# A block-sparse attention and squared-ReLU kernel: new one-hot table, shorter mask chain, a second output bank, and the third query tile of batch 0 masked on VectorE

## The chip, the cores and the metric

The kernel runs on one core of one Trainium2 chip. The metric is the device time of a run in microseconds (us); lower is better. PE is TensorE, ACT is ScalarE, DVE is VectorE, POOL is GpSimd, SP is SyncE, which issues most of the loads.

## The reference

Attention for 4 batches x 8 heads, 768 positions of 64 numbers, under a mask of 32x32 blocks: the band around the diagonal, the first and last block row and column, and three sampled blocks for each block row. Its output, 3072 x 512, goes through two matrices with a squared ReLU between them.

```python
scores = scale * np.matmul(q, k.transpose(0, 1, 3, 2))
...
scores = np.where(mask, scores, -1000000000.0)
scores = scores - np.max(scores, axis=-1, keepdims=True)
attn = np.exp(scores)
attn = attn / (np.sum(attn, axis=-1, keepdims=True) + 1e-09)
...                       # np.matmul(attn, v), then per token:
h = x @ w_in
r = np.maximum(h, 0.0)
g = r * r
return (g @ w_out).astype(np.float32)
```

## The kernel before

A unit is two heads of one batch; a batch has four units. A unit has three query tiles of 256, and a query tile has three key pairs (2 x 128 keys). For each key pair PE makes scores, ACT exponentials `pT`, and PE multiplies them with V into an output bank `po`. After three key pairs ACT takes the inverse of the sums (two Ln, one Exp) and DVE normalises into `xT`. Only then is the bank free. When all four units have normalised a query tile, its hidden matmuls `ph` can run, which fill PE wherever attention leaves it idle.

In batch 0 the mask is not there yet. PE adds it to the scores with four further matmuls a key pair, from a one-hot table `oh` and mask rows `bq`. From batch 1 on, DVE multiplies `pT` with a finished mask.

```python
add = u < HP and qi < NQ_ADD            # NQ_ADD = 3: all of batch 0
for c in range(2 if add else 0):
    for h, hs in enumerate(HALVES):
        nc.tensor.matmul(ps[:, h, c, :], oh[hs, ksl[c]], bq[hs, qsl], start=c == 0, stop=False, ...)
for c in range(2):
    for h, hs in enumerate(HALVES):
        nc.tensor.matmul(ps[:, h, c, :], KT[i][hs, ksl[c]], QT[i][hs, qsl], start=not add, stop=True, ...)
...
otile[u, qi] = ps_o.tile([P, 2, QW], F32, name="po", tag="po")      # one bank: bufs=1
...
def inverse(u, qi):                     # ACT: Ln, Ln, Exp
def normalize(u, qi):                   # DVE: two multiplies out of po; then the bank is free
```

The order of instructions on each engine is not written by hand. The kernel records tasks with assumed durations, landing times and priorities, and a list scheduler in the kernel issues them. So one changed number can move the order of everything after it.

The softmax here doesn't subtract the row's maximum and nothing guards it: scores larger than these inputs give would overflow.

Of the kernel before, what the change touches and what calls it, by code (L numbers as in the profile page):

```python
# [25 lines left out]
def kernel(  # L26
# [94 lines left out]
    def run_schedule(free, bufs, ring):  # L121


        taken = {name: [] for name in bufs}
        left = {e: [t for t in tasks if t.eng == e] for e in free}
        while any(left.values()):
            best = None
            for e, ts in left.items():
                cand = [(max(r, free[e]), t) for t in ts
                        for r in (t.ready(taken, bufs),) if r is not None]  # L130
                if cand:
                    at = min(c[0] for c in cand)
                    t = min((c[1] for c in cand if c[0] <= at + 1e-9), key=lambda t: (t.key, t.order))
                    if best is None or at < best[0]:
                        best = (at, t)
            assert best is not None, "no task can start"
            at, t = best
            t.end = t.issued = free[t.eng] = at + t.us
            if t.dma:
                t.end = ring[t.eng] = max(ring[t.eng], t.end) + t.dma  # L140
            if t.get:
                taken[t.get].extend(t.bufs)
            for p in t.put:
                p.holds -= 1
                p.free = max(p.free or 0.0, t.end + t.late)
            left[t.eng].remove(t)
            t.fn()
        return max(free.values())
# [32 lines left out]
    load_part(nc.sync, 0, 1, 1, CP)  # L181
    load_part(nc.sync, 0, 2, 0, CP)
    load_part(nc.sync, 1, 1, 0, CP)
    load_part(nc.sync, 1, 0, 0, 1)
    load_part(nc.sync, 1, 2, 0, CP)
# [22 lines left out]
    col = consts.tile([nb, nb], F32, name="col")  # L208
    row = consts.tile([nb, 1], F32, name="row")
    small = dict(allow_small_or_imprecise_dtypes=True)  # L210
    G.iota(rel, pattern=[[1, nb]], base=0, channel_multiplier=-1, **small)
    G.iota(col, pattern=[[1, nb]], base=0, channel_multiplier=0, **small)
    G.iota(row, pattern=[[0, 1]], base=0, channel_multiplier=1, **small)


    warm = consts.tile([P, 512], BF, name="warm")
# [3 lines left out]
    def warm_up(n):  # L220
        nc.tensor.matmul(pw[:, 0:n], warm[:, 0:P], warm[:, 0:n], start=True, stop=True)  # L221

    for _ in range(4):
        warm_up(512)
# [4 lines left out]
    key = consts.tile([P, S], mybir.dt.int16, name="key")  # L229
    ends = consts.tile([P, 2], F32, name="ends")  # L230
    oh = consts.tile([P, S], BF, name="oh")
    for hs in HALVES:
        G.iota(ends[hs, 0:1], pattern=[[0, 1]], base=0, channel_multiplier=block, **small)
    G.iota(key[:, 0:2 * P], pattern=[[1, 2], [NCH, P]], base=0, channel_multiplier=0, **small)
    identb = consts.tile([P, P], BF, name="identb")
    make_identity(nc, identb)
    G.iota(key[:, 2 * P:S], pattern=[[1, NCH - 2], [NCH, P]], base=2, channel_multiplier=0, **small)

    def one_hot(n0, n1):
        cols = slice(n0 * P, n1 * P)  # L240
        V.tensor_scalar(out=oh[:, cols], in0=key[:, cols], scalar1=ends[:, 0:1], scalar2=None, op0=AOP.is_ge)
        V.scalar_tensor_tensor(out=oh[:, cols], in0=key[:, cols], scalar=ends[:, 1:2], in1=oh[:, cols],
                               op0=AOP.is_le, op1=AOP.mult)


    sbf = consts.tile([nb, n_rand], F32, name="sbf")
    edge = consts.tile([nb, 2], F32, name="edge")
    pm = ps_h.tile([nb, 4, nb], F32, name="pm", tag="h")
    V.tensor_scalar(out=pm[:, 0, :], in0=rel, scalar1=-1.0, scalar2=None, op0=AOP.is_ge)
    V.scalar_tensor_tensor(out=pm[:, 1, :], in0=rel, scalar=1.0, in1=pm[:, 0, :],  # L250
                           op0=AOP.is_le, op1=AOP.mult)
    V.tensor_scalar(out=edge[:, 0:1], in0=row, scalar1=0.0, scalar2=None, op0=AOP.is_equal)
    V.tensor_scalar(out=edge[:, 1:2], in0=row, scalar1=float(nb - 1), scalar2=None, op0=AOP.is_equal)
    V.tensor_scalar(out=pm[:, 0, :], in0=pm[:, 1, :], scalar1=edge[:, 0:1], scalar2=edge[:, 1:2],
                    op0=AOP.max, op1=AOP.max)
    V.memset(pm[:, 0, 0:1], 1.0)
    V.memset(pm[:, 0, nb - 1:nb], 1.0)
    V.tensor_scalar(out=ends[:, 1:2], in0=ends[:, 0:1], scalar1=float(block - 1), scalar2=None, op0=AOP.add)
    one_hot(0, 2)
    bm = consts.tile([nb, 2, D], BF, name="bm")  # L260
    V.memset(bm, 0.0)
    V.tensor_copy(out=sbf, in_=sb_i.rearrange("q (r two) -> q r two", two=2)[:, :, 0])
    cur = 0
    for r in range(n_rand):
        V.scalar_tensor_tensor(out=pm[:, 1 - cur, :], in0=col, scalar=sbf[:, r:r + 1],
                               in1=pm[:, cur, :], op0=AOP.is_equal, op1=AOP.max)
        cur = 1 - cur
    V.tensor_scalar(out=bm[:, :, 0:nb], in0=pm[:, cur:cur + 1, :].broadcast_to([nb, 2, nb]), scalar1=-1.0,
                    scalar2=-NEG, op0=AOP.add, op1=AOP.mult)
# [6 lines left out]
    def rows_product(qi):  # L276
        pb = ps_y.tile([P, QW], F32, name="pb", tag="y")
# [6 lines left out]
    def mask_product(qi, cp):  # L284
        pq = ps_y.tile([P, 2, QW], F32, name="pq", tag="y")
# [13 lines left out]
    def cast_qk(eng, u, w, c0, c1):  # L299
# [3 lines left out]
        eng.tensor_copy(out=c[:, ns], in_=raw[u][w][:, :, ns, :].rearrange("p t n d -> p n t d"))  # L303
# [74 lines left out]

    def values(u, qi, cp):
        i = u % NPB  # L380
        pT = ptile.pop((u, qi, cp))
        if cp == 0:
            otile[u, qi] = ps_o.tile([P, 2, QW], F32, name="po", tag="po")
# [94 lines left out]
    for u in (2, 3):  # L478
        load_part(nc.sync, u, 1, 0, CP)
        load_part(nc.sync, u, 0, 0, 1)  # L480
        load_part(nc.sync, u, 2, 0, CP)
# [3 lines left out]
    for i in range(HP):  # L485
        init_v(G, i)

    NQ_ADD = 3
# [3 lines left out]
    land_k = [(3.0, 4.4), (6.7,), (9.3,), (12.0,)]  # L492
    land_q = [(3.5, 13.8, 15.3), (7.1, 14.2, 15.7), (9.7, 14.6, 16.1), (12.4, 14.9, 16.5)]
    land_v = [5.6, 8.2, 10.9, 13.5]
# [15 lines left out]
    wu = [Task("PE", 0.2, 1e6, (lambda: warm_up(256)), get=None if i else "po") for i in range(10)]  # L510
# [4 lines left out]
    oh_t = Task("DVE", 1.0, 0.5, (lambda: one_hot(2, NCH)), after=5.6, **SEM)  # L515
    rc = []
    for qi in range(NQ):
        rp = Task("PE", 0.2, -7 if qi == 0 else 12 * qi - 6, (lambda qi=qi: rows_product(qi)), get="y",
                  deps=[oh_t] if qi else [], after=7.0 * qi, **pe)
        rc.append(Task("ACT", 0.4, -7 if qi == 0 else 12 * qi - 6, (lambda qi=qi: rows_copy(qi)), deps=[rp], put=[rp], **SEM))  # L520
    for qi in range(NQ):
        for cp in range(CP):
            s = HP * CP * NQ_ADD + (qi - 2) % NQ * CP + cp - 6
            t = Task("PE", 0.27, s, (lambda a=(qi, cp): mask_product(*a)), deps=[rc[qi]],
                     get="y", after=13.0 + 2.5 * ((qi - 2) % NQ * CP + cp), **pe)
            mk[qi, cp] = Task("DVE", 0.62, s, (lambda a=(qi, cp): mask_copy(*a)), deps=[t], put=[t], **SEM)

    def prepare_first(u):
# [4 lines left out]
        for w, c0, c1, at, s in parts:  # L533
            n = c1 - c0
            a = (u, w, c0, c1)
            on = "POOL" if c0 and not w else "DVE"
            c = Task(on, 0.06 + (0.17 if on == "DVE" else 0.36) * n, s - 6,
                     (lambda a=a, e=G if on == "POOL" else V: cast_qk(e, *a)), get="qc", after=at, **SEM)
# [42 lines left out]
    N_ONE = 72  # L581

    def attend(s, slots):
# [4 lines left out]
        for j, a in enumerate(slots):  # L588
# [4 lines left out]
            if u >= HP or qi >= NQ_ADD:  # L593
                mm = Task("DVE", 0.82, k - 1, (lambda a=a: mask_mul(V, *a)), deps=[ex, mk[qi, cp]], **SEM)
            va = Task("PE", 0.44, k + 2.2, (lambda a=a: values(*a)), deps=[mm] + cv[u] + va_all[-1:],
                      get=None if cp else "po", put=[ex], **pe)
# [10 lines left out]
    while s < len(order):  # L607
        slots = order[s:s + (1 if s < N_ONE else 2)]
# [49 lines left out]
    run_schedule({"PE": 3.0, "DVE": 3.9, "ACT": 3.2, "POOL": 6.2, "SP": 10.5},  # L658
# [32 lines left out]
```

## Time and profile before

| | before |
|---|---|
| median time | 320.81 us (320.67 to 321.29, 3 runs) |
| profiled span | 319.4 us |
| PE, ACT, DVE, POOL busy | 306.7, 226.7, 203.3, 176.9 us |
| first exponential | 8.73 us |
| first hidden matmul | 39.09 us |

A busy PE is not a PE at its peak: matmuls overlap, so the busy time of PE also covers latency. The Trainium skill says so in "Perfetto Trace Analysis", Identifying the Most-Contended Engine: matmul busy time is not a good measure of how close PE is to its peak. The trace agrees: a value matmul is recorded with 0.27 us, while the next one starts after 0.109. I therefore add a second reading, worked out from the trace. Each matmul gets its cost back to back, as spacings in the traces show it: 0.0545 us for a 64-row matmul (scores and mask adds run in pairs), 0.109 for 128 rows by 256 columns, 0.163 by 384, 0.216 by 512, 0.056 for a transpose, and 0.105 for each change between 64-row, 24-row and full-array matmuls. At any moment, the time passed less the cost of all matmuls issued so far is **PE time lost**. Warm-up matmuls and the three row products count as lost. Span is then PE work plus lost time plus about 4 us of tail: for this kernel 296.4 + 19.0 + 4. Each such account rests on one profile of a kernel. In the profiles of x5 and of x7 to x13 below, 31 to 33 of the 384 output matmuls (`py`) have no record; the lost times given for them count each of these at 0.216 us.

The view that I had not shown in the prediction, and should have, is the ACT timeline reduced to the first step of each inverse. It marks one turn of the output bank (start, length):

```profile
15.13 0.38 ACT L398 ACTIVATE ls<-po 64x256 f32<-64x256 f32 x1
21.21 0.38 ACT L398 ACTIVATE ls<-po 64x256 f32<-64x256 f32 x1
27.26 0.38 ACT L398 ACTIVATE ls<-po 64x256 f32<-64x256 f32 x1
32.80 0.38 ACT L398 ACTIVATE ls<-po 64x256 f32<-64x256 f32 x1
```

The inverses, and with them the turns, are 6.08, 6.05 and 5.54 us apart, although a unit holds only 3 x 0.967 + 1.13 = 4.03 us of ACT work.

### The profile page before, as it was taken

Reading aid. Unit: us, or ns where it says so; the run is one execution under the profiler, and the core shown is the slowest. Engines: PE = TensorE matmul, PEld = TensorE weight load, DVE = VectorE, ACT = ScalarE, POOL = GpSimd, SP = SyncE. Lnnn points to the kernel's source line nnn. Section 1 sums busy time; section 2 is a strip of 40 time slices with the busy share of each in tenths; the row PEclk is TensorE's granted clock in tenths of the full one; section 3 lists DMA queues with packets and bytes.
Section 4 is the critical chain, followed back from the end, with each engine's and each line's share of the span. In section 5 each row is a group of like instructions: output and inputs, shape, how many; then the busy total and the mean of one; then the engine's idle time right before and its main releaser. Section 6 shows DMA issues by size and latency. Waiting matters only on the chain.

```text
span 319.4 us, 6150 instructions
## 1 busy us (share of the span) xinstructions
PE 306.7 (96%) x2339; PEld 174.2 (55%) x2339; DVE 203.3 (64%) x369; ACT 226.7 (71%) x362; POOL 176.9 (55%) x227
## 2 busy tenths in 40 slices
PE   6989899999999999999999989999999999999995
PEld 3555466565655545555555545656555655555542
DVE  7644464485886977888896759786667676332200
ACT  2799978885898998778878688796878687311111
POOL 8560533384866636987664538835354445565620
PEclk9999999999999999999999999999999999999999
DMA  7996699117735735735700253620000000000002
GB/s 227 337 210 144 138 180 197 41 27 205 192 90 182 197 77 158 207 74 183 197 33 35 49 184 64 195 57 33 2 35 33 2 34 33 36 33 33 35 33 99
DMA packets 42597, 34.47 MB, mean 108 GB/s; under 512 B 20680, under 2 KB 39624, under 8 KB 42568
## 3 DMA queue, kind: packets, MB, share of 16 engines
q1 hardware_dynamic: 37928, 29.63, 32.4%
q0 software_dynamic: 4224, 4.19, 8.2%
q8 instruction: 18, 0.29, 0.4%
q10 hardware_dynamic: 416, 0.26, 0.3%
q14 instruction: 11, 0.09, 0.1%
HBM read 27.26 MB, written 6.29 MB: 105 GB/s over the span
## 4 chain that ended last, share of the span: by engine, by line
PE 81%; ACT 9%; DVE 6%; issue 4%; DVEq 0%; ACTq 0%
PE ph L426 24%; PE py L456 22%; PE po L389 11%; PE ps L365 10%; PE po L391 9%; ACT pT L371 5%; PE ps L361 3%; DVE pT L376 2%; DVE r L437 1%; ACT ls L399 1%; ACT ls L398 1%; ACT rs L400 1%; PE pw L221 1%; PE pt L314 1%; DVE xT L410 0%
## 5 line engine op out<-in xcount | busy, mean ns | idle before, releaser
L443 POOL TENSOR_TENSOR g<-r 128x384 bf16<-128x384 f32 (+1 forms) x144 | 130.3, 915 | 100.3 <-DVE r L437 73.4
L371 ACT ACTIVATE pT<-ps 128x1024 bf16<-128x1024 f32 x144 | 142.5, 1020 | 35.8 <-PE ps L365 28.7
L426 PE MATMUL ph<-xT,w_in_sb 128*128 128x384 bf16 (+1 forms) x576 | 118.9, 309 | 1.8 <-DVE r L437 1.6
L456 PE MATMUL py<-w_out_sb,g 128*128 128x512 bf16 x384 | 109.2, 379 | 0.7 <-ACT ys L463 0.7
L376 DVE TENSOR_TENSOR pT<-pT,mask 128x1024 bf16<-128x1024 bf16 x108 | 88.5, 834 | 20.4 <-ACT pT L371 19.0
L437 DVE TENSOR_SCALAR r<-ph 128x384 f32<-128x384 f32 (+1 forms) x98 | 49.7, 513 | 50.4 <-PE ph L426 40.1
L426 PEld LDWEIGHTS <-w_in_sb 128*128 128x128 bf16 x576 | 53.3, 98 | 46.3 <-issue 12.1
L389 PE MATMUL po<-pT,VA 128*128 128x256 bf16 x288 | 71.3, 275 | 2.3 <-ACT pT L371 1.6
L391 PE MATMUL po<-pT,VB 128*128 128x256 bf16 x288 | 70.7, 273 | 0.0
L365 PE MATMUL ps<-QT,KT 64*128 64x256 bf16 x576 | 50.4, 274 | 0.0
L456 PEld LDWEIGHTS <-g 128*128 128x128 bf16 x384 | 37.2, 98 | 23.9 <-issue 1.0
L389 PEld LDWEIGHTS <-VA 128*128 128x128 bf16 x288 | 28.0, 97 | 25.9 <-issue 13.9
L435 ACT ACTIVATE r<-ph 128x384 f32<-128x384 f32 (+1 forms) x46 | 20.7, 450 | 23.9 <-POOL g L443 17.1
L365 PEld LDWEIGHTS <-KT 64*128 64x128 bf16 x576 | 22.5, 95 | 20.8 <-issue 18.6
L391 PEld LDWEIGHTS <-VB 128*128 128x128 bf16 x288 | 28.2, 98 | 6.6
L409 DVE TENSOR_TENSOR xT<-po,rs 64x256 bf16<-64x256 f32 x48 | 19.8, 412 | 12.6 <-ACT rs L400 12.4
L398 ACT ACTIVATE ls<-po 64x256 f32<-64x256 f32 x48 | 18.2, 380 | 8.6 <-PE po L391 7.6
L463 ACT COPY ys<-py 128x512 f32<-128x512 f32 x23 | 13.3, 584 | 12.7 <-PE py L456 12.7
L303 POOL CAST qc<-qs 128x768 bf16<-128x768 f32 (+1 forms) x20 | 15.2, 771 | 11.8 <-DMA qs<-in_q_dram 10.1
L400 ACT ACTIVATE rs<-ls 128x256 f32<-128x256 f32 x48 | 20.0, 417 | 1.5
L410 DVE TENSOR_TENSOR xT<-po,rs 64x256 bf16<-64x256 f32 x48 | 20.5, 428 | 0.6
L308 POOL CAST VA<-vs 128x384 bf16<-128x384 f32 x16 | 10.8, 672 | 16.9 <-PE po L389 9.4
(52 smaller groups left out, 116.7 us busy)
## 6 DMA issues: line engine op xcount, KB each, us to landing
vs<-in_v_dram SPq DMA_DIRECT2D x16, 384.0 KB, 5.2
out_dram<-ys SPq DMA_DIRECT2D x23, 256.0 KB, 2.2
ks<-in_k_dram SPq DMA_DIRECT2D x15, 384.0 KB, 4.5
qs<-in_q_dram SPq DMA_DIRECT2D x12, 384.0 KB, 3.6
w_in_sb<-in_moe_w_in_dram POOLq DMA_DIRECT2D x4, 512.0 KB, 10.0
w_out_sb<-in_moe_w_out_dram POOLq DMA_DIRECT2D x4, 512.0 KB, 9.5
qs<-in_q_dram SPq DMA_DIRECT2D x12, 128.0 KB, 5.1
ks<-in_k_dram SPq DMA_DIRECT2D x1, 256.0 KB, 3.1
```

Of the source, the lines that this page charges most:

```text
L365: nc.tensor.matmul(ps[:, h, c, :], KT[i][hs, ksl[c]], QT[i][hs, qsl], start=not add, stop=True, skip_group_check=True)
L371: nc.scalar.activation(out=pT, in_=stile.pop((u, qi, cp)), func=AF.Exp, scale=scale)
L376: eng.tensor_mul(out=pT, in0=pT, in1=mask[:, None, qi, cp * 2:cp * 2 + 2, :].broadcast_to([P, 2, 2, QW]))
L389: nc.tensor.matmul(po[:, 0, :], VA[i][:, n, :], pT[:, 0, c, :], start=first, stop=last, skip_group_check=True)
L391: nc.tensor.matmul(po[:, 1, :], VB[i][:, n, :], pT[:, 1, c, :], start=False, stop=last, skip_group_check=True)
L398: nc.scalar.activation(out=ls[0:D, :], in_=po[D:P, 0, :], func=AF.Ln)
L400: nc.scalar.activation(out=rs, in_=ls, func=AF.Exp, scale=-1.0)
L426: nc.tensor.matmul(ph, w_in_sb[:, kc, f * P:(f + 1) * P], xT[b][:, kc, c0:c0 + w], start=(kc == 0), stop=(kc == KM - 1))
L435: nc.scalar.activation(out=r, in_=htile.pop((T, f)), func=AF.Relu)
L437: V.tensor_scalar(out=r, in0=htile.pop((T, f)), scalar1=0.0, scalar2=None, op0=AOP.max)
L443: G.tensor_mul(out=g, in0=r, in1=r)
L456: nc.tensor.matmul(py, gtile[T, f][:, ts * P:(ts + 1) * P], w_out_sb[:, f, :], start=(f == 0), stop=(f == NF - 1))
```

## The change

It has three parts. *The start*: POOL makes the one-hot table with affine selects, the mask rows take fewer DVE steps, unit 0's first casts go to ACT, more of the warm-up comes first, and K of the next unit is loaded ahead of V of this one. *The bank*: odd units of the first query tile of batch 0 use a second output bank. *The third tile*: the third query tile of batch 0 is masked on DVE (`NQ_ADD` 3 to 2), and six of nine mask products come after 52 us of the scheduler's clock.

```diff
-    load_part(nc.sync, 0, 1, 1, CP)
-    load_part(nc.sync, 0, 2, 0, CP)
+    load_part(nc.scalar, 0, 1, 1, CP)
     load_part(nc.sync, 1, 1, 0, CP)
     load_part(nc.sync, 1, 0, 0, 1)
-    load_part(nc.sync, 1, 2, 0, CP)
+    load_part(nc.sync, 0, 2, 0, CP)
...
     def one_hot(n0, n1):
+        part = oh[HALVES[0], n0 * P:n1 * P]
+        for sign, base in ((1, n0), (-1, block - 1 - n0)):
+            G.affine_select(out=part, in_=part, compare_op=AOP.is_ge, fill=0.0, base=base, ...)
...
-    for r in range(n_rand):
-        V.scalar_tensor_tensor(out=pm[:, 1 - cur, :], in0=col, scalar=sbf[:, r:r + 1], ...)
+    V.tensor_tensor(out=ne, in0=col, in1=sb_i..., op=AOP.not_equal)
+    V.tensor_reduce(out=pm[:, 1, :], in_=ne.rearrange("q r j -> q j r"), op=AOP.min, axis=AX.X)
...
+    def o_pool(u, qi):
+        return "y" if u < HP and u % 2 and qi < NQ_Y else "po"
...
-            otile[u, qi] = ps_o.tile([P, 2, QW], F32, name="po", tag="po")
+            pool, tag = (ps_y, "y") if o_pool(u, qi) == "y" else (ps_o, "po")
+            otile[u, qi] = pool.tile([P, 2, QW], F32, name="po", tag=tag)
...
-    NQ_ADD = 3
+    NQ_ADD = 2
+    NQ_Y = 1
...
-                     get="y", after=13.0 + 2.5 * ((qi - 2) % NQ * CP + cp), **pe)
+                     get="h", after=20.0 + 2.0 * k if k < 3 else 52.0 + 2.0 * k, **pe)
```

Cut: the scheduler's tables of landings and durations, the casts, the loads of units 2 and 3, the fills of V with ones and the warm-up matmuls; also the move of mask and row products from the PSUM pool `y` to the pool `h`, which leaves `y` free to be the second output bank.

More of the change, by code (lines that the diff above doesn't have):

```diff
@@ L137, in run_schedule @@
             at, t = best
-            t.end = t.issued = free[t.eng] = at + t.us
+            t.end = t.issued = free[t.eng] = at + t.us * (2 if t.eng == "PE" and at < COLD else 1)
             if t.dma:
@@ L207 @@
     rel = consts.tile([nb, nb], F32, name="rel")
-    col = consts.tile([nb, nb], F32, name="col")
+    col = consts.tile([nb, n_rand, nb], I32, name="col")
     row = consts.tile([nb, 1], F32, name="row")
     small = dict(allow_small_or_imprecise_dtypes=True)
-    G.iota(rel, pattern=[[1, nb]], base=0, channel_multiplier=-1, **small)
-    G.iota(col, pattern=[[1, nb]], base=0, channel_multiplier=0, **small)
-    G.iota(row, pattern=[[0, 1]], base=0, channel_multiplier=1, **small)
-    warm = consts.tile([P, 512], BF, name="warm")
+    warm = consts.tile([P, QW], BF, name="warm")
@@ L217, with warm_up @@
     V.memset(warm, 0.0)
     pw = ps_o.tile([P, 512], F32, name="pw", tag="po")
-    def warm_up(n):
-        nc.tensor.matmul(pw[:, 0:n], warm[:, 0:P], warm[:, 0:n], start=True, stop=True)
-    for _ in range(4):
-        warm_up(512)
+    def warm_up():
+        nc.tensor.matmul(pw[:, 0:QW], warm[:, 0:P], warm, start=True, stop=True)
+    for _ in range(10):
+        warm_up()
+    G.iota(rel, pattern=[[1, nb]], base=0, channel_multiplier=-1, **small)
+    G.iota(row, pattern=[[0, 1]], base=0, channel_multiplier=1, **small)
@@ L228 @@
+    G.iota(col, pattern=[[0, n_rand], [1, nb]], base=0, channel_multiplier=0, **small)
     HALVES = (slice(0, D), slice(D, P))
-    key = consts.tile([P, S], mybir.dt.int16, name="key")
-    ends = consts.tile([P, 2], F32, name="ends")
     oh = consts.tile([P, S], BF, name="oh")
-    for hs in HALVES:
-        G.iota(ends[hs, 0:1], pattern=[[0, 1]], base=0, channel_multiplier=block, **small)
-    G.iota(key[:, 0:2 * P], pattern=[[1, 2], [NCH, P]], base=0, channel_multiplier=0, **small)
     identb = consts.tile([P, P], BF, name="identb")
-    make_identity(nc, identb)
@@ L237, with one_hot_b @@
-    G.iota(key[:, 2 * P:S], pattern=[[1, NCH - 2], [NCH, P]], base=2, channel_multiplier=0, **small)
+    V.memset(oh[HALVES[0], :], 1.0)
+    V.memset(identb, 0.0)
     def one_hot(n0, n1):
+        part = oh[HALVES[0], n0 * P:n1 * P]
+        for sign, base in ((1, n0), (-1, block - 1 - n0)):
+            G.affine_select(out=part, in_=part, compare_op=AOP.is_ge, fill=0.0, base=base,
+                            pattern=[[sign, n1 - n0], [sign * NCH, P]], channel_multiplier=-sign * block)
+    def one_hot_b(n0, n1):
@@ L240, in one_hot @@
         cols = slice(n0 * P, n1 * P)
-        V.tensor_scalar(out=oh[:, cols], in0=key[:, cols], scalar1=ends[:, 0:1], scalar2=None, op0=AOP.is_ge)
-        V.scalar_tensor_tensor(out=oh[:, cols], in0=key[:, cols], scalar=ends[:, 1:2], in1=oh[:, cols],
-                               op0=AOP.is_le, op1=AOP.mult)
-    sbf = consts.tile([nb, n_rand], F32, name="sbf")
+        V.tensor_copy(out=oh[HALVES[1], cols], in_=oh[HALVES[0], cols])
+    one_hot(0, 2)
+    make_identity(nc, identb, nomemset=True)
@@ L247 @@
+    one_hot(2, NCH)
     edge = consts.tile([nb, 2], F32, name="edge")
-    pm = ps_h.tile([nb, 4, nb], F32, name="pm", tag="h")
-    V.tensor_scalar(out=pm[:, 0, :], in0=rel, scalar1=-1.0, scalar2=None, op0=AOP.is_ge)
+    pm = consts.tile([nb, 2, nb], F32, name="pm")
+    ne = consts.tile([nb, n_rand, nb], F32, name="ne")
+    V.tensor_scalar(out=pm[:, 0, :], in0=rel, scalar1=-1.0, scalar2=None, op0=AOP.is_lt)
     V.scalar_tensor_tensor(out=pm[:, 1, :], in0=rel, scalar=1.0, in1=pm[:, 0, :],
-                           op0=AOP.is_le, op1=AOP.mult)
@@ L252 @@
-    V.tensor_scalar(out=edge[:, 0:1], in0=row, scalar1=0.0, scalar2=None, op0=AOP.is_equal)
-    V.tensor_scalar(out=edge[:, 1:2], in0=row, scalar1=float(nb - 1), scalar2=None, op0=AOP.is_equal)
+                           op0=AOP.is_gt, op1=AOP.max)
+    V.tensor_scalar(out=edge[:, 0:1], in0=row, scalar1=0.0, scalar2=None, op0=AOP.not_equal)
+    V.tensor_scalar(out=edge[:, 1:2], in0=row, scalar1=float(nb - 1), scalar2=None, op0=AOP.not_equal)
     V.tensor_scalar(out=pm[:, 0, :], in0=pm[:, 1, :], scalar1=edge[:, 0:1], scalar2=edge[:, 1:2],
-                    op0=AOP.max, op1=AOP.max)
@@ L256 @@
-    V.memset(pm[:, 0, 0:1], 1.0)
-    V.memset(pm[:, 0, nb - 1:nb], 1.0)
-    V.tensor_scalar(out=ends[:, 1:2], in0=ends[:, 0:1], scalar1=float(block - 1), scalar2=None, op0=AOP.add)
-    one_hot(0, 2)
+                    op0=AOP.min, op1=AOP.min)
+    V.memset(pm[:, 0, 0:1], 0.0)
+    V.memset(pm[:, 0, nb - 1:nb], 0.0)
     bm = consts.tile([nb, 2, D], BF, name="bm")
     V.memset(bm, 0.0)
-    V.tensor_copy(out=sbf, in_=sb_i.rearrange("q (r two) -> q r two", two=2)[:, :, 0])
-    cur = 0
-    for r in range(n_rand):
-        V.scalar_tensor_tensor(out=pm[:, 1 - cur, :], in0=col, scalar=sbf[:, r:r + 1],
-                               in1=pm[:, cur, :], op0=AOP.is_equal, op1=AOP.max)
-        cur = 1 - cur
@@ L268 @@
-    V.tensor_scalar(out=bm[:, :, 0:nb], in0=pm[:, cur:cur + 1, :].broadcast_to([nb, 2, nb]), scalar1=-1.0,
-                    scalar2=-NEG, op0=AOP.add, op1=AOP.mult)
+    one_hot_b(0, 2)
+    init_v(V, 0)
+    V.tensor_tensor(out=ne, in0=col,
+                    in1=sb_i.rearrange("q (r two) -> q r two", two=2)[:, :, 0:1].broadcast_to([nb, n_rand, nb]),
+                    op=AOP.not_equal)
+    V.tensor_reduce(out=pm[:, 1, :], in_=ne.rearrange("q r j -> q j r"), op=AOP.min, axis=AX.X)
+    V.scalar_tensor_tensor(out=bm[:, :, 0:nb], in0=pm[:, 1:2, :].broadcast_to([nb, 2, nb]), scalar=NEG,
+                           in1=pm[:, 0:1, :].broadcast_to([nb, 2, nb]), op0=AOP.mult, op1=AOP.mult)
@@ L276, in rows_product @@
     def rows_product(qi):
-        pb = ps_y.tile([P, QW], F32, name="pb", tag="y")
+        pb = ps_h.tile([P, QW], F32, name="pb", tag="h")
         nc.tensor.matmul(pb, bm.rearrange("a t j -> a (t j)"), oh[0:nb, qi * QW:(qi + 1) * QW], start=True, stop=True)
@@ L284, in mask_product @@
     def mask_product(qi, cp):
-        pq = ps_y.tile([P, 2, QW], F32, name="pq", tag="y")
+        pq = ps_h.tile([P, 2, QW], F32, name="pq", tag="h")
         for c in range(2):
@@ L302, in cast_qk @@
         ns = slice(c0 * 2, c1 * 2)
-        eng.tensor_copy(out=c[:, ns], in_=raw[u][w][:, :, ns, :].rearrange("p t n d -> p n t d"))
+        (eng.copy if eng is nc.scalar else eng.tensor_copy)(
+            out=c[:, ns], in_=raw[u][w][:, :, ns, :].rearrange("p t n d -> p n t d"))
         cast[u, w, c0] = c
@@ L480 @@
         load_part(nc.sync, u, 0, 0, 1)
-        load_part(nc.sync, u, 2, 0, CP)
+        load_part(nc.sync, u - 1, 2, 0, CP)
+    load_part(nc.sync, 3, 2, 0, CP)
     for c in range(1, CP):
@@ L484 @@
             load_part(nc.sync, u, 0, c, c + 1)
-    for i in range(HP):
-        init_v(G, i)
-    NQ_ADD = 3
+    NQ_ADD = 2
+    NQ_Y = 1
+    COLD = 6.5
     PT_BUFS, R_BUFS, G_BUFS, QC_BUFS = 9, 4, 2 * NF + 3, 5
     K_PARTS = {0: [(0, 1), (1, CP)]}
-    land_k = [(3.0, 4.4), (6.7,), (9.3,), (12.0,)]
-    land_q = [(3.5, 13.8, 15.3), (7.1, 14.2, 15.7), (9.7, 14.6, 16.1), (12.4, 14.9, 16.5)]
-    land_v = [5.6, 8.2, 10.9, 13.5]
+    land_k = [(3.05, 4.3), (5.6,), (8.3,), (11.0,)]
+    land_q = [(3.55, 14.6, 16.1), (6.0, 15.0, 16.5), (8.7, 15.4, 16.9), (11.4, 15.8, 17.3)]
+    land_v = [7.2, 9.9, 12.5, 13.7]
     LAT = 0.08
@@ L508 @@
     wl, tr, gate, mk, tp = {}, {}, [], {}, {HP - 1: []}
-    wu = [Task("PE", 0.2, 1e6, (lambda: warm_up(256)), get=None if i else "po") for i in range(10)]
+    wu = [Task("PE", 0.107, 1e6, warm_up, get=None if i else "po") for i in range(16)]
     for a, b in zip(wu, wu[1:]):
@@ L514 @@
     wu[-1].put.append(wu[0].bufs[0])
-    oh_t = Task("DVE", 1.0, 0.5, (lambda: one_hot(2, NCH)), after=5.6, **SEM)
+    oh_t = Task("DVE", 0.2, 0.3, (lambda: one_hot_b(2, NCH)), after=4.2, **SEM)
+    for i in range(1, HP):
+        Task("POOL", 0.8, 0, (lambda i=i: init_v(G, i)), after=4.0 + 2.6 * (i - 1))
     rc = []
     for qi in range(NQ):
-        rp = Task("PE", 0.2, -7 if qi == 0 else 12 * qi - 6, (lambda qi=qi: rows_product(qi)), get="y",
-                  deps=[oh_t] if qi else [], after=7.0 * qi, **pe)
-        rc.append(Task("ACT", 0.4, -7 if qi == 0 else 12 * qi - 6, (lambda qi=qi: rows_copy(qi)), deps=[rp], put=[rp], **SEM))
+        rp = Task("PE", 0.107, -7 if qi == 0 else 6 * qi - 6, (lambda qi=qi: rows_product(qi)), get="h",
+                  deps=[oh_t] if qi else [], after=4.0 if qi == 0 else 7.0 * qi, **pe)
+        rc.append(Task("ACT", 0.37, -7 if qi == 0 else 6 * qi - 6, (lambda qi=qi: rows_copy(qi)), deps=[rp], put=[rp], **SEM))
     for qi in range(NQ):
         for cp in range(CP):
-            s = HP * CP * NQ_ADD + (qi - 2) % NQ * CP + cp - 6
+            k = (qi - NQ_ADD) % NQ * CP + cp
+            s = HP * CP * (NQ_ADD + k // CP) + k % CP - 6
             t = Task("PE", 0.27, s, (lambda a=(qi, cp): mask_product(*a)), deps=[rc[qi]],
-                     get="y", after=13.0 + 2.5 * ((qi - 2) % NQ * CP + cp), **pe)
+                     get="h", after=20.0 + 2.0 * k if k < 3 else 52.0 + 2.0 * k, **pe)
             mk[qi, cp] = Task("DVE", 0.62, s, (lambda a=(qi, cp): mask_copy(*a)), deps=[t], put=[t], **SEM)
@@ L535, in prepare_first @@
             a = (u, w, c0, c1)
-            on = "POOL" if c0 and not w else "DVE"
-            c = Task(on, 0.06 + (0.17 if on == "DVE" else 0.36) * n, s - 6,
-                     (lambda a=a, e=G if on == "POOL" else V: cast_qk(e, *a)), get="qc", after=at, **SEM)
+            on = "POOL" if c0 and not w else "ACT" if u == 0 and not c0 else "DVE"
+            c = Task(on, 0.06 + {"DVE": 0.17, "POOL": 0.36, "ACT": 0.31}[on] * n, s - 6,
+                     (lambda a=a, e={"DVE": V, "POOL": G, "ACT": nc.scalar}[on]: cast_qk(e, *a)), get="qc", after=at, **SEM)
             t = Task("PE", 0.15 * n, s - 5 - w, (lambda a=a: transp(*a)), deps=[c], get="h", put=[c], **pe)
@@ L580 @@
     N_FIRST = HP * NQ_ADD * CP
-    N_ONE = 72
+    PAIRED = lambda s: s >= 72
     def attend(s, slots):
@@ L595, in attend @@
             va = Task("PE", 0.44, k + 2.2, (lambda a=a: values(*a)), deps=[mm] + cv[u] + va_all[-1:],
-                      get=None if cp else "po", put=[ex], **pe)
+                      get=None if cp else o_pool(u, qi), put=[ex], **pe)
             va_all.append(va)
@@ L607 @@
     while s < len(order):
-        slots = order[s:s + (1 if s < N_ONE else 2)]
+        slots = order[s:s + 1 + PAIRED(s)]
         for u, qi, cp in slots:
@@ L656 @@
                     Task("SP", 0.5, 0, (lambda T_=T_, ts=ts: store(T_, ts)), deps=[yc], put=[yc], late=2.0)
-    run_schedule({"PE": 3.0, "DVE": 3.9, "ACT": 3.2, "POOL": 6.2, "SP": 10.5},
+    run_schedule({"PE": 3.3, "DVE": 3.8, "ACT": 3.0, "POOL": 4.3, "SP": 10.5},
                  {"ps": 2, "po": 1, "h": 2, "y": 1, "pT": PT_BUFS, "r": R_BUFS, "g": G_BUFS, "ys": 3,
```

## The prediction

> **What bounds the kernel now.** I read the busy totals first, then the busy times by stretch, then the chain of work that ended last, then the timelines of the first 60 us engine by engine.
>
> ```profile
> PE 306.7 (96%) x2339; PEld 174.2 (55%) x2339; DVE 203.3 (64%) x369; ACT 226.7 (71%) x362; POOL 176.9 (55%) x227
> ```
>
> TensorE (PE) is busy 96% of the span, the others far less, so PE looks like the bound everywhere. The table by stretch (columns: stretch, its length, then busy us and instructions of PE, PEld, DVE, ACT, POOL, clock, DMA share, GB/s) says that this holds only after 40 us.
>
> ```profile
> 16.00:20.00 4.00, 3.34 (x40) 1.86 (x35) 1.50 (x5) 4.00 (x6) 3.62 (x8) 1.00 1.20 212
> 20.00:24.00 4.00, 3.65 (x45) 2.29 (x44) 2.29 (x8) 3.93 (x7) 1.51 (x4) 1.00 1.24 208
> 24.00:40.00 16.00, 14.31 (x152) 7.69 (x152) 6.78 (x14) 14.92 (x22) 4.69 (x7) 1.00 0.66 141
> 40.00:60.00 20.00, 19.96 (x198) 12.27 (x198) 9.95 (x24) 16.08 (x25) 6.90 (x12) 1.00 0.89 166
> 60.00:80.00 20.00, 19.73 (x159) 11.98 (x158) 13.54 (x26) 14.39 (x25) 11.72 (x16) 1.00 0.34 93
> ```
>
> From 16 to 40 us ScalarE (ACT), with the exponentials of batch 0, is the full engine; from 40 us on PE is. So there are three regimes: a start of serial preparation up to the first exponential, an ACT-bound part, and a long PE-bound part. The chain (start, length, what) and the ACT timeline show the start:
>
> ```profile
> 4.20 0.21 DVE bm L268
> 4.45 0.39 PE pb L278
> 4.84 1.39 PE pw L221 x6
> 6.23 0.43 PE pt L314 x4
> 6.66 0.64 PE pw L221 x3
> 7.30 0.43 PE pt L314 x4
> 7.72 0.54 PE ps L361 x4
> 8.27 0.43 PE ps L365 x4
> ```
> ```profile
> 8.73 1.02 ACT L371 ACTIVATE pT<-ps 128x1024 bf16<-128x1024 f32 x1 [3.49 <-PE ps L365]
> ```
>
> VectorE (DVE) works without a pause from 1.16 to 4.40 us on the mask rows, then the chain passes through ten cold PE groups, and the first exponential starts at 8.73. At 7.72 four 64-row matmuls still take 0.54 us; from 10.88 they take 0.33: the array is cold until then. Later, in the PE-bound third query tile of batch 0, the PE and ACT timelines read:
>
> ```profile
> 48.09 0.39 PE L361 MATMUL ps<-bq,oh 64*128 64x256 bf16 x4
> 48.32 0.38 PE L365 MATMUL ps<-QT,KT 64*128 64x256 bf16 x4
> 48.63 0.39 PE L426 MATMUL ph<-xT,w_in_sb 128*128 128x256 bf16 x2
> ```
> ```profile
> 51.47 2.11 ACT L371 ACTIVATE pT<-ps 128x1024 bf16<-128x1024 f32 x2 [0.76 <-PE po L391]
> 53.61 0.38 ACT L398 ACTIVATE ls<-po 64x256 f32<-64x256 f32 x1
> 54.00 0.38 ACT L399 ACTIVATE ls<-po 64x256 f32<-64x256 f32 x1
> 54.41 0.42 ACT L400 ACTIVATE rs<-ls 128x256 f32<-128x256 f32 x1
> 54.73 1.01 ACT L371 ACTIVATE pT<-ps 128x1024 bf16<-128x1024 f32 x1
> 56.49 2.11 ACT L371 ACTIVATE pT<-ps 128x1024 bf16<-128x1024 f32 x2 [0.76 <-PE po L391]
> ```
>
> The gap between starts gives the real PE cost: the four mask-add matmuls (L361) take 48.32 - 48.09 = 0.23, call it 0.22 us (two run at once on the halves of the array), and the four score matmuls 0.31. ACT idles 0.76 us in each 5.02 us unit, waiting for PE.
>
> **What the Trainium skill says.** "TensorEngine Tiling (Array Packing)", Key Properties: changing the tiling mode drains TensorE. The trace agrees: score groups cost 0.31 before a full-array group, where four warm 64-row matmuls alone cost 0.22, so about 0.1 us per change. Therefore a removed add group saves only its 0.22, since it shares its mode with the scores. "TensorE: Matmul & The Clock Gate", What's actually happening: the array runs at half rate until it has been busy some 3.4 us. The trace agrees (0.54 against 0.33 us). The warm-up train of before has a hole from 3.08 to 4.45. "SBUF — State Buffer", Who interferes with whom: a DVE operation with two SBUF inputs contends with a GpSimd (POOL) operation that reads SBUF. The mask multiplies (L376) are of this kind: median 0.693, mean 0.834, longest 1.365 us. "Perfetto Trace Analysis", GPSIMD Engine Instruction: POOL's spans are unreliable, so I put no weight on single affine selects.
>
> **Part 1, the start.** The DVE one-hot steps for the first columns (0.28 + 0.48), the sbf cast (0.28) and three equality steps (3 x 0.25) go. In come two memsets, a copy of 64x256 (est. 0.15), one 24x72 compare and one reduce (est. 0.25 each, from the 0.235 mean of a 24x24 step), and V memsets (est. 0.7 in all). POOL makes the table: the 128x128 select took 0.29 and the 256-column iota 0.35, so two selects of 256 columns are about 0.9, the identity 0.3; begun at 1.5 they are done near 2.7. So the mask rows end near 4.1 to 4.3, hardly sooner than 4.40. The gain is elsewhere: the first K and Q casts move to ACT, which idles from 2.48 to 4.88. Data issued at 0.73 landed 2.3 us later, so K is cast by about 3.4 and Q by 3.95, against 4.59 and 5.1. By the instruction order, eleven warm matmuls fill PE to about 3.5 and only three stand between there and the first scores, against nine. Mask product at 4.3, copy done near 5.05, Q evacuated near 5.2, the 512-column K cast near 4.9 and its four transposes to 5.4, then adds and scores for 1.07 us as now: first exponential at **6.5**, a gain of 2.2. K of units 1 to 3 lands earlier too: V of unit 0 no longer precedes it (1280 KB ahead and itself before, 896 KB after, at about 350 GB/s: 1.1 us), so ACT should not starve behind the earlier start.
>
> **Part 2, batch 0 as a pipeline.** 12 score groups (4 units x 3 key pairs of the third tile) lose 4 matmuls each: 12 x 0.22 = 2.6 us of PE. DVE gains 12 multiplies x 0.7 to 0.83 = 8.4 to 10 us. The values of odd units in the first tile use a second bank, so PE no longer stands behind the normalisation (0.52 us idle at 29.47). I measure progress by the 36th, last exponential of batch 0: it starts at 59.75 now. If ACT alone sets the pace, its spacing of 0.967 us, 9 inverses of 1.13 ahead of it, and 2 later row copies of 0.3 give 35 x 0.967 + 9 x 1.13 + 0.6 = 44.6 us after the first. From 6.5 that is 51.1; with 1.0 us of early stalls (now 1.5) and 1.5 us of others, 53.6. PE's need between the 19th and the 36th score group: 17 x 0.22 + 5 x 0.22 adds + 12 x 0.44 values + 48 hidden x 0.109 + one output pair 0.43 + 34 changes x 0.105 = 19.3 us, against ACT's 21: it fits. Gain at this milestone: **6.1 us**.
>
> **Part 3, what is pushed past the milestone.** By the order, before the 36th score group PE had done 9 mask products, 46 hidden and 4 output matmuls; afterwards 3, 48 and 2. Six products at 0.32 with their changes cost 1.9 and the rest 0.2: **+2.1**. Everything behind is the same work on a PE that is full.
>
> **Part 4, DVE after the milestone.** From 54 to 84 us DVE must do about 16 multiplies (13), six mask copies of 0.69 (4.1), ten relus of 0.42, five normalisations of 0.85 and two K casts: 27 us of 30. It was 13.5 of 20. I allow **+0.7** for multiplies that arrive late. Sum: -6.1 + 2.1 + 0.7 = -3.3, so 320.8 - 3.3 = 317.5 us.
>
> **Rivals.** (1) *Transfers set the start.* Loads run at 320 to 368 GB/s from 4 to 12 us; if K of unit 1 comes late, ACT stops after three exponentials and the 2.2 are mostly lost: about 319.5. Against it: 1.1 us earlier K, and V casts waited for their loads without stopping ACT. (2) *DVE takes the place of PE.* In the third tile alone DVE's load is 12 x 0.834 + 12 x 0.42 + 4 x 0.85 + 0.56 = 19 us, ACT's 16; nine pT buffers let exponentials run ahead, so part is absorbed; if not, PE waits 2 to 3 us and the time is 320. Speaking for it: the contended multiplies. (3) *PE was the bound all along and the filler fits perfectly*: hidden work begins about 8 us sooner, at 31 for 39.1, with 2.5 us more PE work behind it (mask products and mode changes): -5.5, 315.3. Against it: ACT's 21 us leave no room for perfection.
>
> **Range and chances.** The main case has most weight, the three rivals span 315.3 to 320, so 8 in 10 for 315.0 to 320.0. Two per cent faster needs under 314.4, beyond even rival 3: 0.09. Slower by 2% needs a schedule gone wrong: 0.01. Same: 0.90.
>
> **What would show it.** First exponential near 6.5; the first warm scores by about 8; the 36th exponential near 53.6 with ACT over 90% from 16 us to there; hidden matmuls from about 31; six mask products after 52 us; PE busy over 95% from 55 us to the end, and DVE at about nine tenths from 55 to 80. If the first exponential is early but the 10th is not, rival 1 holds; if values wait for mask multiplies, rival 2. I would be wrong altogether if the later part, whose instruction order also changes, lost or won idle PE time (now about 7 us after 40).

## The result

| | before | changed |
|---|---|---|
| median time | 320.74 us (320.32 to 321.29, 4 runs) | 317.14 us (316.91 to 317.93, 4 runs) |
| profiled span | 319.4 us | 315.2 us |
| first exponential | 8.73 | 7.46 |
| 12th exponential | 23.24 | 23.20 |
| 36th exponential, the last of batch 0 | 59.75 | 54.88 |
| first hidden matmul | 39.09 | 32.26 |

The ratio is 0.9891 (95% interval 0.9868 to 0.9914). Ratios here are the mean time of one kernel's fast runs over the mean of the other's in the same rounds, so they are not quite the ratio of the medians quoted.

The busy totals of the changed kernel:

```profile
PE 304.4 (97%) x2303; PEld 171.9 (55%) x2303; DVE 211.2 (67%) x378; ACT 227.3 (72%) x364; POOL 179.2 (57%) x224
```

PE has 36 matmuls fewer (48 mask adds go, 12 short warm-ups come), DVE 8 us more. The table by stretch, columns as in the prediction:

```profile
16.00:20.00 4.00, 4.00 (x48) 2.45 (x47) 0.29 (x1) 3.69 (x7) 4.00 (x9) 1.00 1.05 173
20.00:24.00 4.00, 4.00 (x46) 2.66 (x42) 1.79 (x5) 3.93 (x7) 1.49 (x5) 1.00 1.24 206
24.00:40.00 16.00, 15.60 (x165) 9.12 (x164) 8.22 (x22) 15.67 (x25) 2.88 (x7) 1.00 0.54 125
40.00:60.00 20.00, 19.26 (x166) 10.76 (x166) 17.70 (x33) 17.47 (x25) 16.06 (x20) 1.00 0.83 137
60.00:80.00 20.00, 20.00 (x148) 11.56 (x148) 15.20 (x29) 12.92 (x25) 11.38 (x15) 1.00 0.49 154
```

From 24 to 40 us both PE and ACT are fuller than before; from 40 to 60 us DVE goes from 9.95 to 17.70 us and PE falls to 19.26. The start, in the ACT timeline and in the chain (start, length, what):

```profile
7.46 2.12 ACT L374 ACTIVATE pT<-ps 128x1024 bf16<-128x1024 f32 x2 [1.48 <-PE ps L368]
9.73 1.04 ACT L374 ACTIVATE pT<-ps 128x1024 bf16<-128x1024 f32 x1
11.65 1.02 ACT L374 ACTIVATE pT<-ps 128x1024 bf16<-128x1024 f32 x1 [0.89 <-PE ps L368]
```
```profile
3.30 6.15 DMA ks<-in_k_dram
9.54 0.97 DVE qc L305
10.56 0.51 PE pt L317 x6
11.07 0.33 PE ps L364 x4
```

The first exponential is 1.27 us sooner, but then ACT stalls. The chain says why: PE's queue has the six transposes of unit 2's K ahead of unit 1's scores, and that K lands 6.15 us after it was issued. In the third tile the scores now stand without adds (PE timeline, then ACT timeline):

```profile
52.23 0.39 PE L368 MATMUL ps<-QT,KT 64*128 64x256 bf16 x4
52.55 0.28 PE L397 MATMUL po<-pT,VA 128*128 128x256 bf16 x1
```
```profile
48.60 1.92 ACT L374 ACTIVATE pT<-ps 128x1024 bf16<-128x1024 f32 x2
50.71 3.02 ACT L374 ACTIVATE pT<-ps 128x1024 bf16<-128x1024 f32 x3 [0.19 <-PE ps L368]
```

Scores to the next group take 0.32 us, where adds and scores took 0.54, and ACT's wait of 0.76 us a unit is down to 0.2. The bank turns, each marked by the first step of an inverse in the ACT timeline (start, length):

```profile
19.01 0.38 ACT L406 ACTIVATE ls<-po 64x256 f32<-64x256 f32 x1
22.08 0.38 ACT L406 ACTIVATE ls<-po 64x256 f32<-64x256 f32 x1
25.15 0.38 ACT L406 ACTIVATE ls<-po 64x256 f32<-64x256 f32 x1
27.30 0.38 ACT L406 ACTIVATE ls<-po 64x256 f32<-64x256 f32 x1
```

The first inverse comes 3.9 us later than before, yet the fourth comes 5.5 us sooner, because turns are now 2.2 to 3.1 us apart.

The account of PE time, worked out as described above (us, from the profiles; the last column is the span):

| kernel | PE work | lost to 20 | 20 to 40 | 40 to 60 | 60 to 200 | 200 to 300 | span |
|---|---|---|---|---|---|---|---|
| before | 296.4 | 9.7 | 2.4 | 0.3 | 5.7 | 0.9 | 319.4 |
| changed | 294.0 | 9.8 | 1.0 | 1.3 | 4.1 | 1.0 | 315.2 |

So the 4.2 us of span are 2.4 us of PE work, 1.4 us at 20 to 40 and 1.6 us at 60 to 200, less 1.0 at 40 to 60 and 0.1 each in two other columns. The new start contributes nothing to the time lost by 20 us.

### The profile page after: what moved, and what is told of

It reads as the page before. It is cut to its first block, busy times and chain, and to the rows that moved or that the text cites. A ratio compares the mean times of both kernels' runs of the same rounds, so it can differ in the third digit from the quotient of the medians.

```text
span 315.2 us, 6102 instructions
## 1 busy us (share of the span) xinstructions
PE 304.4 (97%) x2303; PEld 171.9 (55%) x2303; DVE 211.2 (67%) x378; ACT 227.3 (72%) x364; POOL 179.2 (57%) x224
## 4 chain that ended last, share of the span: by engine, by line
PE 82%; DVE 7%; ACT 4%; issue 3%; DMA 2%; SPq 1%; DVEq 0%; ACTq 0%
PE ph L434 25%; PE py L464 24%; PE po L397 10%; PE ps L368 10%; PE po L399 9%; DVE pT L379 4%; ACT pT L374 2%; DVE r L445 2%; DMA ks<-in_k_dram 2%; PE ps L364 2%; PE pq L290 1%; SPq L174 1%; DVE qc L305 1%; ACT ls L407 0%; PE pw L217 0%
## 5 line engine op out<-in xcount | busy, mean ns | idle before, releaser
L379 DVE TENSOR_TENSOR pT<-pT,mask 128x1024 bf16<-128x1024 bf16 x120 | 98.4, 837 | 15.1 <-ACT pT L374 13.5
L368 PEld LDWEIGHTS <-KT 64*128 64x128 bf16 x576 | 21.4, 94 | 23.2 <-issue 21.2
L406 ACT ACTIVATE ls<-po 64x256 f32<-64x256 f32 x48 | 18.3, 381 | 12.5 <-PE po L399 11.6
L311 POOL CAST VA<-vs 128x384 bf16<-128x384 f32 x16 | 11.5, 719 | 15.7 <-PE po L397 10.4
L407 ACT ACTIVATE ls<-po 64x256 f32<-64x256 f32 x48 | 18.1, 376 | 0.6
```

The costliest lines, as they stand in the source:

```text
L379: eng.tensor_mul(out=pT, in0=pT, in1=mask[:, None, qi, cp * 2:cp * 2 + 2, :].broadcast_to([P, 2, 2, QW]))
```

## The experiments

Twelve kernels ran in four to six runs each, beside runs of the kernel before. All gave the right output. The three parts make a factorial table, with ratios to the kernel before:

| | one bank | two banks |
|---|---|---|
| old start, third tile on PE | 1 (before) | 0.9928 (x9) |
| old start, third tile on DVE | 1.0010 (x4) | **0.9826 (x10)** |
| new start, third tile on PE | 1.0002 (x3) | 0.9969 (x1) |
| new start, third tile on DVE | 1.0084 (x2) | 0.9891 (changed) |

The mask products stand at the times of the kernel before in x1, x3, x4 and x9, and at those of the changed kernel in x2 and x10.

**x1, third tile undone.**

```diff
-    NQ_ADD = 2
+    NQ_ADD = 3
...          # and the mask products at the times of the kernel before
```

> The changed kernel with the third query tile of batch 0 masked by TensorE again, and the mask products issued at the times of the kernel before. Main theory (three separate gains: earlier start 1.27 us, third tile off TensorE, second bank): only start and bank remain, so about 318.7 us, 1.5 us slower than the changed kernel's 317.1, and the 36th exponential near 58 us instead of 54.88. Rival (the gain is nearly all the earlier start, the third tile's saving is eaten by the six mask products moved behind it): 317.1 to 317.6.

Measured: 319.61 us (319.34 to 320.35), ratio 0.9969 [0.9954, 0.9984], 36th exponential at 56.63. The third tile is worth 319.61 - 317.14 = 2.5 us in this setting, not the 1.5 of the main theory; the rival is out.

**x2, one bank.**

```diff
-    NQ_Y = 1
+    NQ_Y = 0
```

> The changed kernel with one output bank only. Main theory: values of the second unit stand behind the first unit's normalisation again, twice some 0.3 to 0.5 us: 317.6 to 318.0 us. Rival (the scheduler hides it behind other work): 317.1 within 0.3.

Measured: 323.32 us (322.70 to 324.45), ratio 1.0084 [1.0065, 1.0103]: slower than the kernel before, and 6.2 us slower than the changed kernel. Both theories missed it. The inverses say what happens (ACT timeline):

```profile
19.28 0.38 ACT L406 ACTIVATE ls<-po 64x256 f32<-64x256 f32 x1
24.85 0.38 ACT L406 ACTIVATE ls<-po 64x256 f32<-64x256 f32 x1
30.35 0.38 ACT L406 ACTIVATE ls<-po 64x256 f32<-64x256 f32 x1
```

The first inverse is as late as in the changed kernel and the turns are 5.5 us again. First hidden matmul: 39.21 instead of 32.26. PE loses 4.9 us at 20 to 40 (changed: 1.0), and over the whole run PE's waits are headed by values that wait for exponentials, 3.9 us of it between 20 and 40 us (releaser, total us, times, longest):

```profile
PE po L397 <- ACT pT L374: 4.8, 6, 1.7
```

**x3, start only** (both edits above).

> The changed kernel with both the third tile and the second bank undone, so only the new start is left. Main theory: before less the 1.27 us by which the first exponential came sooner: 319.4 us. Rival 1 (an early start is swallowed by late K loads): 320.3 or more. Rival 3 (the start is most of the gain): 318 or less.

Measured: 320.54 us (320.23 to 322.11), ratio 1.0002 [0.9982, 1.0022]. First exponential 7.45, yet lost by 20 us is 10.1. Rival 1's figure is the one that holds.

**x4, third tile alone on the kernel before.**

```diff
-    NQ_ADD = 3
+    NQ_ADD = 2
```

> The kernel before with one number changed: only two query tiles of batch 0 masked on TensorE, the third on VectorE, and nothing else. Main theory: 2.6 us of TensorE work vanish from a full engine, and the mask products stay early: 318.0 to 318.8 us. Rival (VectorE takes over as the limit of the third tile): 320 or more.

Measured: 321.17 us (320.66 to 321.36), ratio 1.0010 [0.9997, 1.0024]. PE work falls by 2.8 us to 293.6, and lost time rises by 3.0: 1.0 at 40 to 60 and 2.1 at 60 to 200. While PE makes the third tile's scores, the sixth to ninth inverses stand at 43.55, 48.67, 53.52 and 58.94 us, against 43.64, 48.59, 53.61 and 58.62 before. The bank's turns kept their pace, so the freed PE time went to hidden matmuls. The 100th came at 74.36 instead of 79.74 us, but the attention that everything waits for did not move: the 288th value matmul came at 140.20 against 139.78, and by the 300th hidden matmul (174.02 against 173.60) the lead was gone. This is where the expected gain went: into filler done early, with the engine idle later.

**x9, bank alone on the kernel before.** After x1 to x4 I formed a new theory: the loop of one bank paces batch 0.

```diff
-            otile[u, qi] = ps_o.tile([P, 2, QW], F32, name="po", tag="po")
+            pool, tag = (ps_y, "y") if o_pool(u, qi) == "y" else (ps_o, "po")
+            otile[u, qi] = pool.tile([P, 2, QW], F32, name="po", tag=tag)
...          # NQ_Y = 1; mask and row products move from the PSUM pool y to the pool h
```

> The kernel before with only the second output bank for odd units of the first query tile added (mask products moved to the other PSUM pool, as the change does). New theory, from the runs so far: with one bank the loop values, inverse, normalise, next values (5.0 to 6.1 us a unit in the kernel before, 4.1 us of exponentials) paces batch 0, and two banks let the first tile finish sooner, so that the hidden layer's matmuls may start sooner. Then the bank alone, with early first values at 11.4 us, completes the four units of the first tile near 24 to 26 us instead of 34 and gains 1 to 3 us: 318 to 320. Rival: the bank helps only together with the removed mask adds, 320.5 to 321.

Measured: 318.57 us (318.04 to 318.72), ratio 0.9928 [0.9916, 0.9940]. The bank alone gains 2.2 us. The fourth inverse is at 27.14 instead of 32.80. The tile thus ended near 29 us, not at 24 to 26, and the first hidden matmul came at 43.21, later than before: the gain here is that attention runs ahead (288th value matmul at 134.52 against 139.78), not an early filler as I had put it. The move of the products to another pool is not what gains: x3 has it too, without the second bank, and measures 1.0002.

**x10, bank and third tile with the old start.**

> The kernel before with second bank and third tile on VectorE, but with the old start: what is missing to the changed kernel is the new start alone. If the start is worth its 1.27 us: 318.4. If the start is worth nothing even with two banks: 317.1. If the old start is better, since its first values come four us sooner: 316.5 or less.

Measured: 315.23 us (314.71 to 315.59), ratio 0.9826 [0.9812, 0.9840]. **This beats both kernels.** It is 1.9 us faster than the changed kernel, and the two intervals do not overlap. So the new start, taken as a whole, costs time in this setting. Its inverses:

```profile
14.97 0.38 ACT L403 ACTIVATE ls<-po 64x256 f32<-64x256 f32 x1
19.23 0.38 ACT L403 ACTIVATE ls<-po 64x256 f32<-64x256 f32 x1
23.22 0.38 ACT L403 ACTIVATE ls<-po 64x256 f32<-64x256 f32 x1
27.20 0.38 ACT L403 ACTIVATE ls<-po 64x256 f32<-64x256 f32 x1
```

They begin 4 us sooner than in the changed kernel and turn every 4.0 us, which is ACT's own work per unit, so I read the first tile as bound by ACT now. Lost by 20 us: 8.8, against 9.8.

**x8, ones later.**

```diff
-    init_v(V, 0)        # was ahead of the compare with the sampled blocks
...                      # compare, reduce, mask rows
+    init_v(V, 0)
```

> The changed kernel with the two VectorE fills of ones (2 x 0.38 us) moved from before the last three mask steps to after them, so the mask rows end 0.75 us sooner (near 4.5 instead of 5.23 us). If the first exponential sets the pace of batch 0, the time falls by 0.3 to 0.75 us, to 316.4 to 316.8. If the K load of the third unit or the first tile's values set the pace: 317.1 within 0.3.

Measured: 317.36 us (317.07 to 318.05), ratio 0.9897 [0.9882, 0.9912], so within 0.3 of the changed kernel. The last mask step began only 0.28 us sooner (4.75 against 5.03), because the compare itself then took 0.67 us instead of 0.16. In this profile PE ran cold to about 10.2 us and the first exponential came at 8.35. The edit did not move what it was to move, so the run says little about what sets the pace.

**x5, fewer warm-ups.**

```diff
-    for _ in range(10):
+    for _ in range(1):
         warm_up()
```

> The changed kernel with two warm-up matmuls at the start instead of eleven, so TensorE idles from about 1.6 to 3.6 us and runs the start's matmuls at half rate. If the warm array is what brought the first exponential forward (2.23 us from mask rows to exponential against 4.33 in the kernel before): first exponential 0.7 to 2 us later, at 8.2 to 9.5. On the time: 0.5 to 1.5 us slower if the start is on the path, 317.1 within 0.3 if it is not.

Measured: 317.40 us (317.19 to 317.85), ratio 0.9897 [0.9884, 0.9910]; first exponential 8.08. The same row product, at the same moment, in the changed kernel and in x5 (PE timelines):

```profile
5.29 0.28 PE L280 MATMUL pb<-oh,bm 24*128 24x256 bf16 x1 [1.08 <-DVE bm L270]
```
```profile
5.28 0.39 PE L280 MATMUL pb<-oh,bm 24*128 24x256 bf16 x1 [1.06 <-DVE bm L270]
```

The array is warm in the first and cold in the second. But x1, with all eleven warm-ups, has it cold too (0.39 us, first exponential 8.09), while x2 and x3 have it warm at that moment, but cold again from about 7.5 to 10.9 us. So with eleven warm-ups the first exponential comes early in some profiles only, and on the time nothing is measured.

**x11, old order of loads in the new start.**

```diff
     load_part(nc.scalar, 0, 1, 1, CP)
+    load_part(nc.sync, 0, 2, 0, CP)
     load_part(nc.sync, 1, 1, 0, CP)
     load_part(nc.sync, 1, 0, 0, 1)
-    load_part(nc.sync, 0, 2, 0, CP)
+    load_part(nc.sync, 1, 2, 0, CP)
...          # the later units likewise, and the table of landings of the kernel before
```

> The changed kernel with V of each unit loaded ahead of the next unit's K again, as in the kernel before, and the scheduler's table of landings with it; masks, table, casts and warm-up stay new. Theory: the new start costs because V of unit 0 is late (cast at 8.43, first values at 15.48 against 11.35 us), so TensorE has nothing to fill 10 to 15 us with and loses 2.5 us there. Then first values come before 13 us, lost TensorE time at 20 us falls from 9.8 to about 9, and the time to 315.5 to 316.5. Rival (the loss is not in the loads but in how the later order happens to fall): 317.1 within 0.4, or no better lost time at 20 us.

Measured: 315.68 us (314.18 to 316.39, 6 runs), ratio 0.9843 [0.9828, 0.9858], clear of the changed kernel's interval and level with x10. First values at 13.33 us (changed: 15.48), lost by 20 us 8.8: the theory's figures, apart from the first values, which came 0.3 us after its bound. (The profile is of the fastest run, 314.18 us; the six runs scatter over 2.2 us.) So what costs in the new start is V loaded behind K, together with the table that goes with it. The two were not tried apart, and x7 below shows that the table alone can move the time by as much.

**x7, true landings.**

```diff
-    land_k = [(3.05, 4.3), (5.6,), (8.3,), (11.0,)]
+    land_k = [(3.05, 4.3), (6.0,), (9.4,), (11.9,)]
...          # land_q and land_v likewise
```

> The changed kernel with the scheduler told the landing times that the trace shows (K of unit 2 at 9.4 us instead of 8.3, V of unit 0 at 8.4 instead of 7.2, and so on); the loads themselves are unchanged. If the loss at 10 to 15 us comes from transposes that stand in TensorE's queue ahead of scores and wait for a late K: ACT's stalls of 1.9 us before 17 us fall under 1 us, and the time by 0.3 to 1.0. If the loss is that V is late, nothing is won: 317.1 within 0.4.

Measured: 319.03 us (318.57 to 320.89), ratio 0.9953 [0.9933, 0.9974]: slower by 1.9 us, which neither side expected. Its profile fell in the cold phase (first exponential 8.09, second at 10.11). ACT waited 3.5 us for scores between 7 and 20 us, and the first hidden matmul came at 37.68. It shows only that the landings that the trace shows do not make a better order by themselves. It decides nothing between the two theories.

**x12, the second bank in two tiles**, on x10.

```diff
-    NQ_Y = 1
+    NQ_Y = 2
```

> The kernel before with second bank and third tile on VectorE (315.23 us) and the second bank used in the second query tile as well. If the loop of one bank (5.5 to 6.2 us between inverses from 31 us on) still costs: 0.5 to 1.0 us faster, 314.3 to 314.8. If the hidden layer already fills TensorE there: 315.2 within 0.4.

Measured: 316.78 us (316.64 to 317.38), ratio 0.9879 [0.9866, 0.9893]: 1.5 us slower than x10. The turns in the second tile do fall to 4.0 us (30.78, 34.76, 38.73, 42.71), but PE loses as much by 60 us as in x10 (10.6 against 11.2) and more at 60 to 200 (5.1 against 3.4). Faster turns there buy nothing that lasts. Why the later order is worse is open.

**x13, mask products early.**

```diff
-    ... after=20.0 + 2.0 * k if k < 3 else 52.0 + 2.0 * k, **pe)
+    ... after=20.0 + 2.0 * k, **pe)
```

> The changed kernel with all nine mask products from 20 us on, two us apart, instead of six of them after 52 us. The prediction's part 3 charged 2.1 us for pushing them back. If that charge was real: 315.0 to 316.0. If TensorE has no idle time left at 20 to 40 us (lost there: 1.0 us in all), moving them wins nothing: 316.8 to 317.6.

Measured: 317.40 us (317.09 to 317.52), ratio 0.9892 [0.9878, 0.9907]: nothing. The first hidden matmul moved from 32.26 to 43.00 us: the products took the places of hidden matmuls. That the time stayed shows that the first hidden matmul is no measure of the gain.

## Why the prediction was right or wrong

The number was right: 317.5 predicted, 317.14 measured, chances included. The sum behind it was not. Several terms failed and cancelled, so that it came within 0.4 us is partly luck. Measured along one path through the table, from the kernel before over x9 and x10 to the changed kernel, the 3.6 us are 2.2 of the bank and 3.3 of the third tile, less 1.9 for the new start.

*Part 1, "first exponential at 6.5, a gain of 2.2"*: it came at 7.46 in the profile. The mask rows began their last step at 5.03 us, not ended by 4.3; the small estimates were short (the fill of `oh` took 0.70 us, the copy 0.43, two 24x24 steps 0.40 and 0.39), and Q landed so late that its cast began at 4.42, when it should have ended by 3.95. In other profiles of the same start the array stayed cold and the first exponential came at 8.1. More than the size failed: the step took a sooner first exponential for a sooner everything. With one bank the start is worth nothing (x3), and with two banks and the third tile it costs 1.9 us (x10 against the changed kernel). It costs as well with two banks alone (x9 to x1: ratio 0.9928 to 0.9969) and with the third tile alone (x4 to x2: 1.0010 to 1.0084, where the times of the mask products differ too). The sentence that failed is "K of units 1 to 3 lands earlier too ... so ACT should not starve". K did come earlier (the casts of units 1 and 2 begin at 6.53 and 9.54 us, before at 8.74 and 11.48), but ACT starved more: between the first exponential and 17 us it waited 1.7 us for scores, before 0.8. PE's queue held unit 1's scores behind the K of unit 2, which the scheduler's table expected at 8.3 us and which landed near 9.5; V of unit 0 was cast at 8.43 instead of 6.93, and by the 12th exponential the lead was down to 0.04 us. The first rival described this outcome; I gave it too little weight.

*What bounds the kernel now, "From 16 to 40 us ScalarE (ACT) ... is the full engine"*: ACT's 14.92 of 16 us is true, but ACT was running ahead into buffers: the 12th exponential, the last of the first tile, began at 23.24 us and that tile's last inverse at 32.80. The bank loop, 5.5 to 6.1 us a unit, set when the first tile ended. The Trainium skill warns of it in one line: "consistent bubbles can mean SBUF/PSUM ran out" ("Trainium Kernel Development and Optimization", Best Practices). The inverses of x9 and x10 agree, with turns of 4.0 us once there are two banks.

*Part 2, the bank term "0.52 us idle at 29.47"*: mis-sized. It is worth 2.2 us alone (x9) and 6.2 us at the end of the row (x2 against the changed kernel). *Part 2, "12 x 0.22 = 2.6 us of PE"*: right in size where the bank is doubled, 2.5 us (x1 against changed) and 3.3 us (x9 against x10); without the second bank it is nothing (x4), which the prediction did not see. The milestone, the 36th exponential, moved by 59.75 - 54.88 = 4.9 us for 6.1, and nearly all of it by the bank: it stands at 55.73 in x9, at 60.06 in x4 and at 61.74 in x3. Hidden matmuls began at 32.26 for "about 31".

*Part 3, "+2.1" for mask products pushed back*: not borne out; moved early they win nothing (x13), and they did not hold up the milestone either: it stands at 55.91 in x13 and at 55.85 in x5, which began as cold but has the products late. That they cost the same PE time wherever they stand on a full engine is my reading. *Part 4, "+0.7" for DVE*: near in size, not in kind. PE loses 1.0 us at 40 to 60 us, where DVE is busy 17.70 of 20 us, and mask multiplies still average 0.837 us against a median of 0.693. But no value waited for a late multiply there: PE's one wait for DVE in that stretch is a hidden matmul behind a relu, 0.42 us, and from 60 to 200 us its waits for multiplies sum to 0.2. So the second rival did not come true. From the milestone on, 4.9 shrank to 4.2 us of span, so 0.7 was given back, not 2.8.

*Still open*: the kernel before loses 5.7 us at 60 to 200 us, the changed one 4.1, x10 3.4 and x12 5.1, with nearly the same instructions in another order. Among the waits in that stretch are hidden matmuls behind relus (before, 1.6 us) and values behind normalisations (changed, 1.3 us), but no run separates what in the order makes them.

## What to carry to other kernels

When one engine fills its gaps with independent work, ask which loop hands that work over, and time that loop by its turns, not by busy shares. A single accumulator that must be normalised before reuse can be the bound while two engines look full. A saving in a stage paced by such a loop can turn into filler done early and be lost later, as in x4, and parts of a change should be timed in all combinations: here the best kernel leaves out one of the three.

## What the Trainium skill lacked or had wrong

- "TensorEngine Tiling (Array Packing)", Key Properties, says that a change of tiling mode drains TensorE but gives no cost. Here it is about 0.1 us: four scores take 0.32 us to the next full-array group, where four 64-row matmuls alone take 0.22.
- "TensorE: Matmul & The Clock Gate", What's actually happening, puts the warm-up at some 3.4 us of activity, calls the window free-running, and names an idle window of that length for the way back. The free-running part agrees: after the same matmuls from 1.12 to 4.21 us and a gap of 1.1 us, the array was warm at 5.29 us in the changed kernel's profile and cold in x1's (0.28 against 0.39 us for one row product). The way back does not: in x2 four mask adds take 0.39 us at 6.80, 0.61 at 8.17 and 0.39 again at 11.27, and the granted clock from 7.6 to 10.9 us is 0.50, although PE was busy for 1.74 of the 3.3 us before that. x3 does the same after 1.67 of 3.3 us. How much idling is enough, the section does not say.
- No page that I read gives the time of an affine select on POOL: two of 64x256 bf16 took 0.91 us, two of 64x512 took 1.32 us, one of 128x128 took 0.28 us, in spans that the profile calls rough.
- "Perfetto Trace Analysis", Matmuls, advises that independent groups rotate through PSUM banks, but no page that I read works out the turn time of one output bank (values, inverse, normalisation) as a bound of its own. In the first tile it is 5.5 to 6.1 us with one bank in the kernel before, and 2.2 to 4.3 us with two (changed kernel, x10); the second bank is worth 2.2 to 6.2 us of 320.
